# Hedgehog attention and a gated MLP on one core: one pool of PSUM banks, and the stages of a unit moved against each other

## The chip, the cores and the metric

One core of a Trainium2 chip runs the whole kernel in one launch. The metric is the device time of one execution in microseconds, as the median of several runs. TensorE (PE) multiplies matrices into PSUM; VectorE (DVE) and ScalarE (ACT) read PSUM and work elementwise; GpSimd (POOL) works on SBUF and issues the loads that convert fp32 to bf16; SyncE (SP) issues the other transfers.

## What is computed

The reference, cut to what matters (8 batches, 8 heads, 576 positions, 64 values per head, 128 features, all fp32):

```python
def phi(x):
    proj = x @ w_phi
    proj = proj - max(abs(proj), axis=-1)
    return concatenate([exp(proj), exp(-proj)])
kv  = einsum('bhsf,bhsd->bhfd', phi(k), v);  z = sum(phi(k), axis=2)
x   = (phi(q) @ kv) / (phi(q) @ z + 1e-06)         # heads side by side: (8, 576, 512)
h   = relu(x @ w_in);  u, v2 = h[..., :512], h[..., 512:]
v_s = w_spatial @ layernorm(v2) + b_spatial[:, None]
out = (u * v_s) @ w_out
```

## The kernel before

The 576 positions of a batch are 512 in four blocks of 128 and a rest of 64; the rests of two batches share one block. The attention is cut into 36 **units**: for each two batches one unit for their rests (a tail unit, all 8 heads), then four units per batch, each for two heads ("pairs"). Each unit goes through these stages, written as functions:

- `a_transpose` (L182): 8 transposes on TensorE of key and query blocks into one bank; ScalarE copies the key half to `kT` (L194), VectorE the query half to `qT` (L195), one after the other.
- `a_keys` (L204): the key features, two banks of `ps`. VectorE takes the largest magnitude, `mk` (L212), then ScalarE the exponentials `kf` (L215), four in all.
- `a_queries` (L217): the same product for the queries, of which only the largest magnitude `mq` is kept (L221).
- `a_scale` (L224): ScalarE makes `em` = exp(-mk), exp(mk) (L227); GpSimd multiplies the values by it into `vs` (L232, two instructions, and a small copy L234; L242 and L244 in a tail unit).
- `a_split` (L248): two small VectorE instructions write `mq` as a bf16 value (L250) and its remainder (L251) into `mhl`.
- `a_max_t` (L253): `mhl` is transposed (L255) and VectorE copies it to `mT` (L256).
- `a_qfeat` (L258): the query features transposed, less their maximum (L266 and L270, which reads `mT`), and their exponentials `qf` on ScalarE (L283).
- `a_kv` (L286): the key sums (L296, L298), copied to `kv` by VectorE (L300).
- `a_num` (L308): numerator and denominator (L315), then reciprocal and product on VectorE (L305, L306).
- `a_x_t` (L319): the result transposed (L324) and copied to `xT` (L325).

The MLP of a batch is a list of **fillers** made by `b_tasks` (L482), each about four wide matmuls and what reads them: `b_v` (L372: product, ReLU on ScalarE, statistics on VectorE L362), `b_ln` (L383: root on GpSimd, four normalisations L387), `b_u` (L403: product, ReLU on ScalarE), `b_s` (L423: spatial product, gate on VectorE L431), `b_o` (L456: product, copy on ScalarE L453, store). There are 160 of them in all. A batch's list enters the queue when `a_x_t` of its last unit is emitted.

The order is written out by hand in `step(i)` (L513): one call emits stages of up to four units, and `fill(0.25)` four times, each adding a quarter of RATE to a credit (at most 2) and emitting one filler per credit. From this order the building tool makes one program per engine, in which each engine works strictly in turn; it may change the order a little where it takes an instruction to be ready earlier. What is left in the queue after the last step is emitted at the end (L567), the **drain**.

Before, a step emits for the units u (this one), w, z, y (one, two, three before): transposes of u, fill, `mT` of w, key sums of w, keys of u, fill, `xT` of y, queries of u, query features of w, fill, numerators of z, scale and split of u, fill. PSUM has 8 banks, in four pools: 1 for every transpose (`ps_tr`), 3 for feature products (`ps_pj`), 2 for key sums and numerators (`ps_kn`), 2 for the MLP (`ps_s2`). The spatial weights are transposed on TensorE after units 4 and 5 (L157).

Loads with conversion are issued on GpSimd (L84, L97, L98, L121 to L124), the fp32 values on SyncE (L86, L99). The identity that every transpose needs is built on GpSimd (L108, L109; masks.py:197 and 199).

Of the kernel before, what the change touches and what calls it, by code (L numbers as in the profile page):

```python
# [16 lines left out]
def kernel(  # L17
# [15 lines left out]
    nc = tc.nc  # L33
# [24 lines left out]
    ps_tr = ctx.enter_context(tc.tile_pool(name="ps_tr", bufs=1, space=bass.MemoryType.PSUM))  # L58
    ps_pj = ctx.enter_context(tc.tile_pool(name="ps_pj", bufs=3, space=bass.MemoryType.PSUM))
    ps_kn = ctx.enter_context(tc.tile_pool(name="ps_kn", bufs=2, space=bass.MemoryType.PSUM))  # L60
    ps_s2 = ctx.enter_context(tc.tile_pool(name="ps_s2", bufs=2, space=bass.MemoryType.PSUM))
# [43 lines left out]
    nc.gpsimd.dma_start(out=wphi2[D:2 * D, F:2 * F], in_=w_phi)  # L105
    load_tail(0)
    load(0, parts=4)
    ident = cpool.tile([P, P], BF16)  # L108
    make_identity(nc, ident)  # L109
# [4 lines left out]
    wsp = cpool.tile([P, NB, S], BF16)  # L114
# [5 lines left out]
    def load_weights():  # L120
        nc.gpsimd.dma_start(out=w_in_bf, in_=moe_w_in.rearrange("(kc p) f -> p kc f", p=P))  # L121
        nc.gpsimd.dma_start(out=wsp, in_=moe_w_spatial[0:T0, :].rearrange("(p c) s -> p c s", c=NB))
# [34 lines left out]
    def transpose_spatial(i):  # L157

        pt = ps_tr.tile([P, S], BF16, tag="tr", name="pt")
# [9 lines left out]
        for bl in range(2):  # L169
            lo = bl * TL  # L170
            for tp, c in enumerate(POS):
                nc.tensor.transpose(out=pt[lo:lo + TL, tp * P:(tp + 1) * P], in_=wsp[:, c, T0:S], identity=ident)
# [9 lines left out]
    def a_transpose(u):  # L182
        src = st[u["b"]] if u["pair"] else gs[u["g"]]
        pt = ps_tr.tile([P, 2, 4, P], BF16, tag="tr", name="pt")
# [12 lines left out]
    def by_token(xT, half):  # L197
        ps = ps_pj.tile([P, 4, F], FP32, tag="pj", name="ps")
# [5 lines left out]
    def a_keys(u):  # L204
# [3 lines left out]
                            bufs=3 if u["pair"] else 2)  # L208
# [15 lines left out]
    def a_scale(u):  # L224
# [3 lines left out]
        if u["pair"]:  # L228
            pj = u["pj"]
            vs = feat.tile([P, 2, H, DS], BF16, tag="vs", name="vs", bufs=3)  # L230
# [22 lines left out]
    def a_max_t(u):  # L253
        pt = ps_tr.tile([P, P], BF16, tag="tr", name="pt")
        nc.tensor.transpose(out=pt, in_=mhl[u["i"] % NM], identity=ident)  # L255
        nc.vector.tensor_copy(out=mT[u["i"] % NM][0:2 * H, :], in_=pt[0:2 * H, :])  # L256

    def a_qfeat(u):  # L258
# [3 lines left out]
        for half in range(2):  # L262
            pq = ps_pj.tile([P, 4, P], FP32, tag="pj", name="pq")
# [14 lines left out]
            if u["pair"]:  # L278
                qf = feat.tile([P, 2, 4, P], BF16, tag="qf", name="qf", bufs=5)
# [6 lines left out]
    def a_kv(u):  # L286
# [4 lines left out]
        pv = ps_kn.tile([P, 2, 2, DA], FP32, tag="kn", name="pv")  # L291
# [16 lines left out]
    def a_num(u):  # L308
        d = st[u["b"]]
        u["x"] = a1.tile([P, NB, 2, D], BF16, tag="x", name="x", bufs=3)  # L310
        for hh in range(2):
            pn = ps_kn.tile([P, NB, DA], FP32, tag="kn", name="pn")
# [6 lines left out]
    def a_x_t(u):  # L319
        if u["pj"] == 0:  # L320
            st[u["b"]]["xT"] = s2.tile([P, KC, T0], BF16, tag="xT", name="xT", bufs=3)
        pt = ps_tr.tile([P, NB, P], BF16, tag="tr", name="pt")
# [4 lines left out]
    def tail_num(g, bls):  # L327
# [4 lines left out]
        for i in range(2):  # L332
            pn = ps_kn.tile([P, 4, DA], FP32, tag="kn", name="pn")
# [265 lines left out]
```

## Time and profile before

| | us |
|---|---|
| median of 3 runs | 374.42 |
| the runs | 373.71 to 376.15 |
| the profiled execution | 374.99 |
| its span in the trace | 373.2 |

| engine | busy us | share of the span |
|---|---|---|
| TensorE matmuls | 301.4 | 81% |
| VectorE | 280.4 | 75% |
| ScalarE | 235.1 | 63% |
| GpSimd | 138.5 | 37% |

The span runs from the first to the last instruction; the execution's time is 1.8 us longer. Matmuls overlap in their pipeline, so TensorE's busy time is somewhat more than its work. VectorE is called DVE in the rows, ScalarE ACT, GpSimd POOL.

### The profile page before, as it was taken

The numbers are of one execution on the slowest core, as the hardware profiler recorded it, in microseconds if no ns is written. First come the engines' busy times: TensorE is split into PE (matmuls) and PEld (weight loads), VectorE is DVE, ScalarE is ACT, GpSimd is POOL, SyncE is SP. The second block draws the span as 40 slices with busy tenths as digits, with TensorE's granted clock in tenths as the row PEclk, the third lists the DMA queues.
The fourth block names the chain that finished last, engine by engine and source line by source line (L and its number), as shares of the span: only waits on it lengthen the run. The fifth ranks groups of instructions, "written<-read, shape, count | busy, mean of one in ns | idle before, by whom it ended". The sixth has DMA issues, their size and how long they took to land.

```text
span 373.2 us, 8490 instructions
## 1 busy us (share of the span) xinstructions
PE 301.4 (81%) x3370; PEld 201.3 (54%) x3370; DVE 280.4 (75%) x696; ACT 235.1 (63%) x514; POOL 138.5 (37%) x198
## 2 busy tenths in 40 slices
PE   0176768796988799879787999897868998898995
PEld 0055656564655566546554667565536665554442
DVE  5288868898866988599987997788797985567260
ACT  3058635875677686777866667877776558651633
POOL 7669522454603632434425230635332222220010
PEclk9999879998999999999998999999999999999998
DMA  8999980088112931373009301990000003210303
GB/s 184 215 202 202 104 184 2 2 112 142 27 62 70 115 114 50 90 103 114 2 1 114 115 1 58 180 246 3 0 2 3 0 4 138 97 23 0 129 0 126
DMA packets 44460, 31.13 MB, mean 83 GB/s; under 512 B 14018, under 2 KB 39170, under 8 KB 44420
## 3 DMA queue, kind: packets, MB, share of 16 engines
q0 software_dynamic: 26624, 11.71, 25.4%
q1 hardware_dynamic: 17796, 18.88, 16.0%
q8 instruction: 26, 0.43, 0.5%
q14 instruction: 14, 0.11, 0.1%
HBM read 32.85 MB, written 9.44 MB: 113 GB/s over the span
## 4 chain that ended last, share of the span: by engine, by line
PE 23%; DVE 17%; ACT 13%; POOL 8%; DMA 4%; issue 3%; POOLq 0%; ACTq 0%; DVEq 0%; SPq 0%
ACT kf L215 5%; PE po L451 4%; ACT qf L283 4%; PE ps L428 4%; DMA out_dram<-ob 4%; DVE stats L362 3%; POOL vs L232 3%; DVE mk L212 3%; DVE vn L387 2%; PE pv L296 2%; POOL rstd L369 2%; PE ps L200 2%; ACT kT L194 1%; PE pv L359 1%; PE pq L266 1%
## 5 line engine op out<-in xcount | busy, mean ns | idle before, releaser
L215 ACT ACTIVATE kf<-ps 128x512 bf16<-128x512 f32 x144 | 75.0, 603 | 54.1 <-DVE mk L212 46.7
L232 POOL TENSOR_TENSOR vs<-v_f,em 128x512 bf16<-128x512 f32 x64 | 65.5, 1044 | 112.1 <-ACT em L227 109.0
L283 ACT ACTIVATE qf<-pq 128x512 bf16<-128x512 f32 x128 | 66.6, 621 | 7.8 <-PE pq L270 7.8
L221 DVE TENSOR_REDUCE mq<-ps 128x4 f32<-128x512 f32 x72 | 47.4, 678 | 3.0 <-PE ps L200 1.7
L212 DVE TENSOR_REDUCE mk<-ps 128x4 f32<-128x512 f32 x72 | 47.0, 675 | 1.1 <-PE ps L200 1.1
L296 PE MATMUL pv<-vs,kf 128*128 128x65 bf16 x512 | 26.2, 193 | 21.7 <-POOL vs L234 16.1
L296 PEld LDWEIGHTS <-kf 128*128 128x128 bf16 x512 | 24.1, 97 | 31.1 <-issue 27.1
L194 ACT COPY kT<-pt 128x512 bf16<-128x512 bf16 x36 | 22.3, 620 | 24.2 <-PE pt L191 24.2
L407 PE MATMUL pu<-xT,w_in_bf 128*128 128x512 bf16 x128 | 36.1, 395 | 0.6 <-ACT vr L361 0.6
L428 PE MATMUL ps<-w_spT,vn 128*128 128x512 bf16 x128 | 34.5, 379 | 1.7 <-ACT uTt L421 0.9
L361 ACT ACTIVATE vr<-pv 128x512 bf16<-128x512 f32 (+1 forms) x38 | 22.5, 616 | 18.5 <-PE pv L359 18.3
L362 DVE BATCH_NORM_STATS2 stats<-vr 128x6 f32<-128x512 bf16 (+1 forms) x38 | 25.4, 683 | 11.7 <-ACT vr L361 11.5
L453 ACT COPY ob<-po 128x512 f32<-128x512 f32 (+1 forms) x38 | 22.9, 613 | 17.5 <-PE po L451 10.0
L451 PE MATMUL po<-w_out_bf,uT 128*128 128x512 bf16 x128 | 33.0, 378 | 0.9 <-DVE uT L431 0.5
L359 PE MATMUL pv<-w_in_bf,xT 128*128 128x512 bf16 x128 | 32.5, 379 | 0.8 <-ACT vr L361 0.6
L200 PE MATMUL ps<-wphi,qT 128*128 128x256 bf16 x144 | 29.7, 291 | 3.4 <-ACT kf L215 2.7
L266 PE MATMUL pq<-qT,wphi 128*128 128x256 bf16 x128 | 30.7, 276 | 1.6 <-DVE mq L221 1.3
L270 PE MATMUL pq<-mT,sel 128*128 128x128 bf16 x256 | 30.5, 221 | 0.0
L270 PEld LDWEIGHTS <-sel 128*128 128x128 bf16 x256 | 25.2, 99 | 6.4 <-issue 3.1
L200 PE MATMUL ps<-wphi,kT 128*128 128x256 bf16 x144 | 25.9, 297 | 2.9 <-ACT kT L194 2.9
L431 DVE TENSOR_TENSOR uT<-ps,uT 128x512 bf16<-128x512 f32 x32 | 21.8, 684 | 7.5 <-PE ps L429 7.5
L409 ACT ACTIVATE uT<-pu 128x512 bf16<-128x512 f32 x32 | 19.7, 626 | 10.8 <-PE pu L407 10.8
(107 smaller groups left out, 623.2 us busy)
## 6 DMA issues: line engine op xcount, KB each, us to landing
v_f<-in_v_dram SPq DMA_DIRECT2D x8, 1024.0 KB, 6.8
out_dram<-ob SPq DMA_DIRECT2D x32, 256.0 KB, 2.4
k_bf<-in_k_dram POOLq DMA_DIRECT2D x7, 512.0 KB, 6.5
q_bf<-in_q_dram POOLq DMA_DIRECT2D x7, 512.0 KB, 7.6
v_tl<-in_v_dram SPq DMA_DIRECT2D x8, 128.0 KB, 10.6
w_in_bf<-in_moe_w_in_dram POOLq DMA_DIRECT2D x1, 1024.0 KB, 13.2
out_dram<-ob SPq DMA_DIRECT2D x8, 128.0 KB, 2.3
wsp<-in_moe_w_spatial_dram POOLq DMA_DIRECT2D x1, 576.0 KB, 15.3
```

What stands on the lines that cost most here:

```text
L200: nc.tensor.matmul(out=ps[:, 2 * x:2 * x + 2, :], lhsT=xT[:, 2 * half + x, :], rhs=wphi2, start=True, stop=True)
L212: nc.vector.tensor_reduce(out=u["mk"][:, hs], in_=pk, axis=AX.X, op=ALU.max, apply_absolute_value=True)
L215: nc.scalar.activation(out=u["kf"][:, s, hs, :], in_=pk, func=AF.Exp, bias=0.0, scale=sc)
L221: nc.vector.tensor_reduce(out=u["mq"][:, 4 * half:4 * half + 4], in_=pq, axis=AX.X, op=ALU.max, apply_absolute_value=True)
L232: nc.gpsimd.tensor_tensor(out=vs[:, s, :, 0:D], in0=st[u["b"]]["v"][:, pj * H:(pj + 1) * H, :], in1=em[:, s, :].unsqueeze(2).to_broadcast( ...
L270: nc.tensor.matmul(out=pq[:, 2 * par + x, :], lhsT=sel[:, j, :], rhs=m, start=False, stop=(x == 1))
L283: nc.scalar.activation(out=qf[:, s], in_=pq, func=AF.Exp, bias=0.0, scale=sc)
L296: nc.tensor.matmul(out=pv[:, hh, s, :], lhsT=u["kf"][:, s, 4 * hh + c, :], rhs=u["vs"][:, s, 4 * hh + c, 0:DA], start=(c == 0), stop=False)
L359: nc.tensor.matmul(out=pv[r], lhsT=lhs(kc), rhs=w_in_bf[:, kc, HALF:DFF], start=(kc == 0), stop=(kc == KC - 1))
L362: nc.vector.bn_stats(out=stats[r], in_=dst[r])
L428: nc.tensor.matmul(out=ps, lhsT=d["vn"][:, sp, cs], rhs=w_spT[:, sp, 0:T0], start=(sp == 0), stop=False)
L451: nc.tensor.matmul(out=po[r], lhsT=lhs(dc), rhs=w_out_bf[:, dc, :], start=(dc == 0), stop=(dc == KC - 1))
```

## The change

All PSUM tiles come from one pool with one tag and eight buffers, handed out in turn. `step` emits stages of up to six units, n (the next one) to x (four before): keys and scale of u, fill, key sums of z (two before; until now one before), queries and split of u, fill, transposes of n, `mT` of w, fill, `xT` of x, query features of w, fill, numerators of y. So the transposes come one step earlier, and the key sums, the numerators, `xT` and with it a batch's fillers one step later; there is one step more. RATE falls from 4.4 to 4.0. `kf`, `vs` and `qf` get one, one and two buffers more; the spatial weights use a buffer of `vn` until that is needed, and their last 64 columns are a load of their own. The identity is built ahead of the first loads.

```diff
-    ps_tr = ctx.enter_context(tc.tile_pool(name="ps_tr", bufs=1, space=bass.MemoryType.PSUM))
-    ps_pj = ctx.enter_context(tc.tile_pool(name="ps_pj", bufs=3, space=bass.MemoryType.PSUM))
-    ps_kn = ctx.enter_context(tc.tile_pool(name="ps_kn", bufs=2, space=bass.MemoryType.PSUM))
-    ps_s2 = ctx.enter_context(tc.tile_pool(name="ps_s2", bufs=2, space=bass.MemoryType.PSUM))
+    psum = ctx.enter_context(tc.tile_pool(name="psum", bufs=8, space=bass.MemoryType.PSUM))
...
+    ident = cpool.tile([P, P], BF16)
+    make_identity(nc, ident)
     load_tail(0)
     load(0, parts=4)
-    ident = cpool.tile([P, P], BF16)
-    make_identity(nc, ident)
...
-    wsp = cpool.tile([P, NB, S], BF16)
+    wsp = s2.tile([P, NB, T0], BF16, tag="vn", name="wsp", bufs=3)
+    wspr = cpool.tile([P, NB, TL], BF16)
...
-        nc.gpsimd.dma_start(out=wsp, in_=moe_w_spatial[0:T0, :].rearrange("(p c) s -> p c s", c=NB))
+        rows = moe_w_spatial[0:T0, :].rearrange("(p c) s -> p c s", c=NB)
+        nc.gpsimd.dma_start(out=wsp, in_=rows[:, :, 0:T0])
+        nc.gpsimd.dma_start(out=wspr, in_=rows[:, :, T0:S])
...
-                nc.tensor.transpose(out=pt[lo:lo + TL, tp * P:(tp + 1) * P], in_=wsp[:, c, T0:S], identity=ident)
+                nc.tensor.transpose(out=pt[lo:lo + TL, tp * P:(tp + 1) * P], in_=wspr[:, c, :], identity=ident)
...
-        pt = ps_tr.tile([P, 2, 4, P], BF16, tag="tr", name="pt")
+        pt = psum.tile([P, 2, 4, P], BF16, tag="bank", name="pt")
...
-        ps = ps_pj.tile([P, 4, F], FP32, tag="pj", name="ps")
+        ps = psum.tile([P, 4, F], FP32, tag="bank", name="ps")
...
-                            bufs=3 if u["pair"] else 2)
+                            bufs=4 if u["pair"] else 2)
...
-            vs = feat.tile([P, 2, H, DS], BF16, tag="vs", name="vs", bufs=3)
+            vs = feat.tile([P, 2, H, DS], BF16, tag="vs", name="vs", bufs=4)
...
-                qf = feat.tile([P, 2, 4, P], BF16, tag="qf", name="qf", bufs=5)
+                qf = feat.tile([P, 2, 4, P], BF16, tag="qf", name="qf", bufs=7)
...
-    RATE = 4.4
+    RATE = 4.0
...
     def step(i):
-        u, w, z, y = unit(i), unit(i - 1), unit(i - 2), unit(i - 3)
+        n, u, w, z, y, x = (unit(i + d) for d in (1, 0, -1, -2, -3, -4))
+        if i == 0:
+            a_transpose(u)
         if u:
-            a_transpose(u)
+            a_keys(u)
+            a_scale(u)
         fill(0.25)
+        if z and z["pair"]:
+            a_kv(z)
+        if u:
+            a_queries(u)
+            a_split(u)
+        fill(0.25)
+        if n:
+            a_transpose(n)
         if w:
             a_max_t(w)
-        if w and w["pair"]:
-            a_kv(w)
-        if u:
-            a_keys(u)
+        fill(0.25)
+        if x and x["pair"]:
+            a_x_t(x)
+            if x["pj"] == NP - 1:
+                g, bl = x["g"], x["b"] % 2
+                alone = g in SPLIT
+                if alone or bl == 1:
+                    tail_x_t(g, [bl] if alone else [0, 1])
+                queue.extend(b_tasks(x["b"]))
+        if w:
+            a_qfeat(w)
         fill(0.25)
         if y and y["pair"]:
-            a_x_t(y)
+            a_num(y)
             if y["pj"] == NP - 1:
                 g, bl = y["g"], y["b"] % 2
                 alone = g in SPLIT
                 if alone or bl == 1:
-                    tail_x_t(g, [bl] if alone else [0, 1])
-                queue.extend(b_tasks(y["b"]))
-        if u:
-            a_queries(u)
-        if w:
-            a_qfeat(w)
-        fill(0.25)
-        if z and z["pair"]:
-            a_num(z)
-            if z["pj"] == NP - 1:
-                g, bl = z["g"], z["b"] % 2
-                alone = g in SPLIT
-                if alone or bl == 1:
                     tail_num(g, [bl] if alone else [0, 1])
-        if u:
-            a_scale(u)
-            a_split(u)
-        fill(0.25)
-
-    for i in range(NU + 3):
+
+    def on_pair(i):
+        u = unit(i)
+        return u if u and u["pair"] else None
+
+    for i in range(NU + 4):
         u = unit(i)
         step(i)
         if i == 0:
```

The same edit from the four old pools to `psum.tile(..., tag="bank")` stands at every PSUM tile. `on_pair` is not called.

**Three places in the engines' programs.** First GpSimd at the very start; `k_tl` and `q_tl` are the rest blocks of the first two batches, `k_bf` and `q_bf` full blocks. Before:

```order
L98 DMA q_bf<-in_q_dram 128x2x256
L97 DMA k_bf<-in_k_dram 128x2x256
L98 DMA q_bf<-in_q_dram 128x2x256
masks.py:197 MEMSET ident 128x128
L97 DMA k_bf<-in_k_dram 128x8x256
masks.py:199 ISA
masks.py:199 AFFINE_SELECT ident<-ident 128x128
L98 DMA q_bf<-in_q_dram 128x8x256
L121 DMA w_in_bf<-in_moe_w_in_dram 128x4x1024
```

Now:

```order
L599 UNCONDITIONAL_BRANCH
masks.py:197 MEMSET ident 128x128
L81 DMA k_tl<-in_k_dram 64x8x64
L101 DMA wphi_76<-in_w_phi_dram 64x128
L102 DMA wphi_76<-in_w_phi_dram 64x128
masks.py:199 ISA
masks.py:199 AFFINE_SELECT ident<-ident 128x128
L81 DMA k_tl<-in_k_dram 64x8x64
L81 DMA q_tl<-in_q_dram 64x8x64 x2
L94 DMA k_bf<-in_k_dram 128x2x256
```

The identity moved ahead of all loads but one; behind the loads of batch 1, where `w_in_bf` and the spatial weights were issued before, the tail unit's `vst` now comes first.

Second, VectorE through one unit in the middle, while gates (`uT`, a filler's work) are due. Before:

```order
L212 TENSOR_REDUCE mk<-ps 128x4 x2
L325 COPY xT<-pt 128x512
L221 TENSOR_REDUCE mq<-ps 128x4 x2
L305 RECIPROCAL rc<-pn 128x4 x2
L306 TENSOR_TENSOR x<-pn,rc 128x4x64 x2
L250 CAST mhl_129<-mq 128x8
L251 TENSOR_TENSOR mhl_129<-mq,mhl_129 128x8
L431 TENSOR_TENSOR uT<-ps,uT 128x512
L195 COPY qT<-pt 128x512
L431 TENSOR_TENSOR uT<-ps,uT 128x512
L256 COPY mT_131<-pt 16x128
```

Now:

```order
L212 TENSOR_REDUCE mk<-ps 128x4 x2
L431 TENSOR_TENSOR uT<-ps,uT 128x512
L300 CAST kv<-pv 128x4x65
L221 TENSOR_REDUCE mq<-ps 128x4 x2
L431 TENSOR_TENSOR uT<-ps,uT 128x512
L250 CAST mhl_129<-mq 128x8
L195 COPY qT<-pt 128x512
L251 TENSOR_TENSOR mhl_129<-mq,mhl_129 128x8
L256 COPY mT_127<-pt 16x128
```

The reciprocals and products (`rc`, `x`) stood between `mq` and the two split instructions (`mhl`) and now come after `mT`, outside this piece; `kv` moved up between `mk` and `mq`. In all 35 units that can be compared `mT` stood behind `qT`; now it does in 16 of 34, as here, and ahead of it in 18.

Third, ScalarE through one unit. Before:

```order
L215 ACTIVATE kf<-ps 128x512 x4
L453 COPY ob<-po 128x512
L283 ACTIVATE qf<-pq 128x512 x4
L453 COPY ob<-po 128x512
L227 ACTIVATE em<-mk 128x8 x2
```

Now:

```order
L215 ACTIVATE kf<-ps 128x512 x4
L227 ACTIVATE em<-mk 128x8 x2
L409 ACTIVATE uT<-pu 128x512
L421 ACTIVATE uTt<-pu 128x4x64
L194 COPY kT<-pt 128x512
L283 ACTIVATE qf<-pq 128x512 x4
```

In 14 of the 36 units other instructions stood between the key exponentials (`kf`) and `em`, for which GpSimd waits, in nine of them the query exponentials (`qf`) as here; now `em` follows `kf` directly in all 36.

## Rows read from the trace of the kernel before

**Rows 1.** Busy us by stretch: length, then PE, PEld, DVE, ACT, POOL; granted clock, DMA, GB/s.
```profile
18.30:84.40 66.10, 51.40 (x590) 38.37 (x590) 55.53 (x126) 44.21 (x101) 34.99 (x49) 0.92 0.79 115
84.40:315.50 231.10, 201.01 (x2377) 137.05 (x2377) 189.54 (x474) 161.93 (x362) 82.81 (x115) 0.99 0.31 69
315.50:373.20 57.70, 48.01 (x397) 25.05 (x395) 27.96 (x72) 25.92 (x50) 8.32 (x14) 0.98 0.20 69
```

**Rows 2.** Timeline of ScalarE, the copy of a transposed key block (L194).
```profile
18.30 0.58 ACT L194 COPY kT<-pt 128x512 bf16<-128x512 bf16 x1 [14.56 <-PE pt L191]
...
84.41 0.62 ACT L194 COPY kT<-pt 128x512 bf16<-128x512 bf16 x1
...
315.48 0.72 ACT L194 COPY kT<-pt 128x512 bf16<-128x512 bf16 x1
```

**Rows 3.** Who VectorE waited for, 84.4 to 315.5 us: total us, times, longest.
```profile
DVE qT L195 <- ACT kT L194: 10.5, 11, 3.4
DVE mT L256 <- PE pt L255: 5.6, 9, 1.6
```

**Rows 4.** Who TensorE waited for in the same stretch.
```profile
PE pv L296 <- POOL vs L234: 8.5, 7, 2.3
```

**Rows 5.** Timeline of the start, GpSimd and then TensorE; columns: start us, us, engine, line.
```profile
14.85 0.71 POOL L98 DMA_DIRECT2D q_bf<-in_q_dram  x1 [0.67 <-DMA q_tl<-in_q_dram]
...
16.89 0.30 POOL masks.py:199 TENSOR_SCALAR_AFFINE_SELECT ident<-ident 128x128 bf16<-128x128 bf16 x1
...
18.84 0.55 POOL L122 DMA_DIRECT2D wsp<-in_moe_w_spatial_dram  x1
...
26.83 0.26 POOL L244 CAST vst<-em 64x16 bf16<-64x16 f32 x1
17.25 0.58 PE L191 MATMUL pt<-ident,k_tl 128*128 128x128 bf16 x4 [17.25 <-POOL ident masks.py:199]
```

**Rows 6.** DMA issues on the page: count, KB each, us to landing.
```profile
wsp<-in_moe_w_spatial_dram POOLq DMA_DIRECT2D x1, 576.0 KB, 15.3
```

**Rows 7.** Groups by line: busy us, mean ns of one, then idle before.
```profile
L362 DVE BATCH_NORM_STATS2 stats<-vr 128x6 f32<-128x512 bf16 (+1 forms) x38 | 25.4, 683 | 11.7 <-ACT vr L361 11.5
...
L250 DVE CAST mhl<-mq 128x8 bf16<-128x8 f32 x36 | 17.7, 492 | 0.4
...
L251 DVE TENSOR_TENSOR mhl<-mq,mhl 128x8 bf16<-128x8 f32 x36 | 15.7, 435 | 0.7
```

**Rows 8.** All instructions of L250 and of L251: ns minimum/median/maximum.
```profile
L250 DVE CAST mhl<-mq x36: 154/204/2226, 22.8 to 321.7; 128x8 bf16<-128x8 f32 x36
L251 DVE TENSOR_TENSOR mhl<-mq,mhl x36: 130/168/1000, 23.6 to 321.9; 128x8 bf16<-128x8 f32 x36
```

**Rows 9.** Timeline of one unit in mid-run: VectorE, ScalarE, GpSimd.
```profile
219.27 0.43 DVE L300 CAST kv<-pv 128x260 bf16<-128x260 f32 x1
219.62 1.28 DVE L212 TENSOR_REDUCE mk<-ps 128x4 f32<-128x512 f32 x2
...
225.09 0.42 DVE L306 TENSOR_TENSOR x<-pn,rc 128x256 bf16<-128x256 f32 x1
...
220.33 2.06 ACT L215 ACTIVATE kf<-ps 128x512 bf16<-128x512 f32 x4 [2.39 <-DVE mk L212]
...
222.57 2.04 POOL L232 TENSOR_TENSOR vs<-v_f,em 128x512 bf16<-128x512 f32 x2 [6.00 <-ACT em L227]
```

**Rows 10.** Timeline of one unit near the start, VectorE and then GpSimd.
```profile
33.16 2.23 DVE L250 CAST mhl<-mq 128x8 bf16<-128x8 f32 x1
...
33.28 2.07 POOL L232 TENSOR_TENSOR vs<-v_f,em 128x512 bf16<-128x512 f32 x2
```

**Rows 11.** Timeline of TensorE near the end.
```profile
321.23 0.27 PE L266 MATMUL pq<-qT,wphi 128*128 128x256 bf16 x1
...
322.11 0.66 PE L315 MATMUL pn<-kv,qf 128*128 128x65 bf16 x16
...
345.16 3.63 PE L451 MATMUL po<-w_out_bf,uT 128*128 128x512 bf16 x16 [0.27 <-DVE uT L431]
```

More of the change, by code (lines that the diff above doesn't have):

```diff
@@ L157, in transpose_spatial @@
     def transpose_spatial(i):
-        pt = ps_tr.tile([P, S], BF16, tag="tr", name="pt")
+        pt = psum.tile([P, S], BF16, tag="bank", name="pt")
         if i < NB:
@@ L253, in a_max_t @@
     def a_max_t(u):
-        pt = ps_tr.tile([P, P], BF16, tag="tr", name="pt")
+        pt = psum.tile([P, P], BF16, tag="bank", name="pt")
         nc.tensor.transpose(out=pt, in_=mhl[u["i"] % NM], identity=ident)
@@ L262, in a_qfeat @@
         for half in range(2):
-            pq = ps_pj.tile([P, 4, P], FP32, tag="pj", name="pq")
+            pq = psum.tile([P, 4, P], FP32, tag="bank", name="pq")
             if u["pair"]:
@@ L290, in a_kv @@
         ut = dg["unit"]
-        pv = ps_kn.tile([P, 2, 2, DA], FP32, tag="kn", name="pv")
+        pv = psum.tile([P, 2, 2, DA], FP32, tag="bank", name="pv")
         for hh in range(2):
@@ L311, in a_num @@
         for hh in range(2):
-            pn = ps_kn.tile([P, NB, DA], FP32, tag="kn", name="pn")
+            pn = psum.tile([P, NB, DA], FP32, tag="bank", name="pn")
             for pos in range(NB):
@@ L321, in a_x_t @@
             st[u["b"]]["xT"] = s2.tile([P, KC, T0], BF16, tag="xT", name="xT", bufs=3)
-        pt = ps_tr.tile([P, NB, P], BF16, tag="tr", name="pt")
+        pt = psum.tile([P, NB, P], BF16, tag="bank", name="pt")
         for pos in range(NB):
@@ L332, in tail_num @@
         for i in range(2):
-            pn = ps_kn.tile([P, 4, DA], FP32, tag="kn", name="pn")
+            pn = psum.tile([P, 4, DA], FP32, tag="bank", name="pn")
             for y in range(4):
@@ L348, in tail_x_t @@
         r = slice(bls[0] * TL, (bls[-1] + 1) * TL)
-        pt = ps_tr.tile([P, KC, P], BF16, tag="tr", name="pt")
+        pt = psum.tile([P, KC, P], BF16, tag="bank", name="pt")
         for kc in range(KC):
@@ L356, in v_mm @@
     def v_mm(lhs, dst, r, stats, mv):
-        pv = ps_s2.tile([P, HALF], FP32, tag="s2", name="pv")
+        pv = psum.tile([P, HALF], FP32, tag="bank", name="pv")
         for kc in range(KC):
@@ L404, in b_u @@
         d = st[b]
-        pu = ps_s2.tile([P, T0], FP32, tag="s2", name="pu")
+        pu = psum.tile([P, T0], FP32, tag="bank", name="pu")
         for kc in range(KC):
@@ L415, in b_u_tail @@
         r = slice(bls[0] * TL, (bls[-1] + 1) * TL)
-        pu = ps_s2.tile([P, KC, P], FP32, tag="s2", name="pu")
+        pu = psum.tile([P, KC, P], FP32, tag="bank", name="pu")
         for dc in range(KC):
@@ L424, in b_s @@
         d = st[b]
-        ps = ps_s2.tile([P, T0], FP32, tag="s2", name="ps")
+        ps = psum.tile([P, T0], FP32, tag="bank", name="ps")
         cs = slice(dc * P, (dc + 1) * P)
@@ L434, in b_s_tail @@
         d = gs[g]
-        ps = ps_s2.tile([P, KC, 2, TL], FP32, tag="s2", name="ps")
+        ps = psum.tile([P, KC, 2, TL], FP32, tag="bank", name="ps")
         for dc in range(KC):
@@ L448, in o_mm @@
     def o_mm(lhs, r):
-        po = ps_s2.tile([P, DM], FP32, tag="s2", name="po")
+        po = psum.tile([P, DM], FP32, tag="bank", name="po")
         for dc in range(KC):
```

## The prediction

> **What bounds the kernel now.** I read the copies of the key block first, because each marks the start of a unit's keys: the tail unit's at 18.3, the tenth unit's at 84.4, the last unit's at 315.5 us [rows 2]. These cut the span into a start, a start-up with few fillers, a steady part of 26 units (231.1 / 26 = 8.89 us each) and an end. The busy times by stretch come next [rows 1]. In the steady part TensorE is busy for 201.0 of 231.1 us (87%) and VectorE for 189.5 (82%), ScalarE for 70%: no engine is full, so the units' handovers set the pace, and VectorE and TensorE share the floor. In the end TensorE has 48.0 of 57.7 us and VectorE 28.0, so there TensorE sets the time. Then the waits: VectorE stood 10.5 us at `qT` for ScalarE's copy and 5.6 us at `mT` [rows 3]; TensorE stood 8.5 us at the key sums for GpSimd's `vs` [rows 4]. The sum below goes by VectorE through start-up and steady part, and by TensorE in the end.
>
> **Start.** The last of the tail's query blocks has landed by 14.85 us, where GpSimd's wait for it ends; the first transpose waits until 17.25 us for the identity [rows 5]. With the identity built ahead, the load issues slip by its two pieces, 0.30 us for the one shown and as much for its memset, an estimate: 14.85 + 0.6 = 15.45. From the first transpose to the key copy it took 18.30 - 17.25 = 1.05 us, so that copy comes at 16.5 us, 1.8 earlier. What is late next is the load itself. It cannot gain over 2.4 (17.25 - 14.85), and loses nothing unless the loads slip by over 2.4.
>
> **Start-up.** Up to the tenth unit VectorE was busy for 55.5 us in 66.1 [rows 1]. The fillers now begin a step later and the transposes come a step earlier, so of the seven fillers that stood here none is left. They hold five statistics and four normalisations, some ten instructions at 0.68 us [rows 7] with the small ones, 6.5 us. That leaves 49.0. Of the 10.6 us idle I keep 6.5, since without fillers nothing stands beside a unit's own chain; 3 and 10.6 are the ends. The tenth copy then falls at 16.5 + 49.0 + 6.5 = 72.0 instead of 84.4.
> The spatial weights are issued behind the tail's `vst` now, which ended near 27.1 us [rows 5]; 1.8 earlier and behind `w_in_bf` that makes some 26 instead of 18.8, and with 15.3 us to landing [rows 6] 41. Five units at about 5.5 us from 16.5 put their first use at 42 to 44, so I take nothing; a stall there of up to 4 us stays in the range, and TensorE, in order, would hold every stage behind it.
>
> **Steady part: fillers.** By the rule of credits 107 fillers were emitted between these two copies, and now 103. Of seventeen fillers of a batch the VectorE instructions are four statistics, four normalisations and four gates, 12 x 0.68 / 17 = 0.5 us per filler. So VectorE has 189.5 - 2 = 187.5 us of today's work.
>
> **Steady part: the port.** The two split instructions last 0.492 and 0.435 us in the mean but 0.204 and 0.168 in the median [rows 7, 8]: 0.56 us per unit is standing. One of 2.23 us lies beside GpSimd's 2.07 us of `vs`, and both end together [rows 10]. `vs` began 222.57 - 219.62 = 2.95 us after the first `mk` and lasted 2.04 [rows 9]. Now `em` always follows `kf` directly, and on VectorE the split comes after `mk`, `kv` and `mq`, with 1.28 + 0.43 + 1.28 (`mq` taken as `mk`) = 3.0 us of work: it arrives just as `vs` begins. Before, `rc` and `x` stood between, or `em` was late, and many pairs missed it. The ends are a pair that always misses (27 x -0.56 = -15) and one that always stands as the worst did, 2.23 + 0.17 - 0.93 = 1.47 more, 27 x 1.47 = +40. I take +0.6 per unit, +16 us, nearer to the mean than to the worst, because fillers still shift the pair.
> The Trainium skill (SBUF — State Buffer, "Who interferes with whom") speaks against the change here: a VectorE cast in its two-port mode and a GpSimd instruction lock each other out of a shared pair of ports for a whole instruction, and a VectorE instruction with two SBUF inputs contends with GpSimd's reads too. The trace agrees, as the 2.23 beside 2.07 us shows [rows 10]. By that rule alone, with every pair in the window, the case is the second rival below.
>
> **Steady part: what VectorE waits for.** It was idle for 231.1 - 189.5 = 41.6 us. The waits at `qT` and `mT` are 16.1 of it [rows 3]. The transposes have half a step's lead now, and `mT` no longer stands behind `qT` in 18 of 34 units, so I take 12 of the 16.1 away. While VectorE stands at the port the others catch up: of the 29.6 left I let the 16 added us swallow 15.6, and 14 us remain. Ends: 5, and 35 if the handovers only change places. TensorE's waits for `vs` [rows 4] end too, as the key sums come a step later; with VectorE as the floor that is worth nothing more.
> The one pool adds a wait: a bank comes round after eight tiles, and TensorE, in order, holds transposes, features, numerators and fillers behind it, and so VectorE and ScalarE. No row shows such a ring. Its price lies between nothing and one pair of exponentials per unit (2.06 / 2 = 1.03 [rows 9], 27.8 us); I take nothing, because a unit with its fillers takes 16 banks, so that eight are half a unit's time, over 4 us, and a bank's readers need 0.64 + 1.03 for two exponentials behind `mk`.
> Together 187.5 + 16 + 14 = 217.5 us, 8.37 per unit.
>
> **End.** After the last key copy 46 fillers were left, now 57. A wide product takes 3.63 / 4 = 0.91 us [rows 11], and TensorE sets the time here: 57.7 + 11 x 0.91 = 67.7. The ends are 64 and 70.
>
> **The sum.** 72.0 + 217.5 + 67.7 = 357.2 of span, and 1.8 outside it: 359.0 against the profiled 374.99. The median stands 0.6 below that, so 358.4; I forecast 358.
>
> **Rivals.**
> 1. The port costs no more than today and VectorE is fed almost without a gap. For it: eight banks and a full step of lead. Against it: the order that puts the pair at the window. Start-up 70, steady 187.5 + 13, end 67.7, 1.8, less 0.6: 339.
> 2. The port takes everything: +40, with 5 us of idle left, is 232.5 in the steady part; 72.0 + 232.5 + 67.7 + 1.8 - 0.6 = 373. For it speaks the match of 3.0 and 2.95 us; against it that fillers come between. A cadence that does not change at all comes to much the same, 372.
> 3. Slower: a closed loop through five instruction streams. Where `mT` stands behind the split, it waits for the end of `vs`, 2.95 + 2.04 = 4.99 us after `mk` [rows 9]; then the second split instruction 0.17, query features and numerators 322.11 + 0.66 - 321.23 = 1.54 [rows 11], a filler 0.91, two products 0.84 [rows 9], and the next `mk`: 8.45, with handovers near 8.9, and 9.6 when a second filler's product stands in TensorE's way. It decides from about 18 units of 26 at 9.6: 18 x 9.6 + 8 x 8.37 = 240, and 72.0 + 240 + 67.7 + 1.2 = 381. Against it: `mT` stands ahead of `qT` in half the units.
>
> **How the numbers follow.** Forecast 0.50, first rival 0.25, second 0.15, third 0.10. About 1% can be told from no change (runs 373.7 to 376.2). The forecast's own spread, steady 206 to 228, is 347 to 369, faster throughout; the first rival is faster too; the second falls within 1% but for 0.04 on its fast side; of the third 0.02 falls within 1%. Faster 0.79, same 0.13, slower 0.08. The range reaches down to the first rival and up over the second: 338 to 374.
>
> **What would show it.** In the profile after: first key copy near 16.5, tenth near 72, last near 290 us; VectorE's idle time between the last two under 20 us; the means of the split instructions together near 1.5 us instead of 0.93; no wait for `vs` at the key sums; an end of 66 to 69 us. A tenth copy after 78, a cadence of 8.8 or more, or TensorE waiting for banks by over 10 us in total would make it wrong.

## The result and the profile after

The changed kernel takes 346.25 us in the median of 4 runs (344.78 to 347.78), the kernel before 374.06: a ratio of 0.925, 95% interval 0.919 to 0.930, 28 us faster. Forecast were 358 us in a range of 338 to 374. The profiled execution took 347.78 us and its span is 346.0, against 374.99 and 373.2.

The copies of the key block cut the span as before: the first, the tenth, the eleventh and the last (rows 2 had the first, tenth and last). Columns: start, us, engine, line, idle before.

```profile
15.56 0.58 ACT L194 COPY kT<-pt 128x512 bf16<-128x512 bf16 x1 [11.83 <-PE pt L191]
...
61.59 0.58 ACT L194 COPY kT<-pt 128x512 bf16<-128x512 bf16 x1 [0.94 <-PE pt L255]
73.84 0.62 ACT L194 COPY kT<-pt 128x512 bf16<-128x512 bf16 x1
...
278.55 0.58 ACT L194 COPY kT<-pt 128x512 bf16<-128x512 bf16 x1 [0.21 <-PE pt L255]
```

The engines' busy times by stretch, in the columns of [rows 1], after:

```profile
15.50:61.60 46.10, 35.90 (x487) 28.73 (x486) 41.87 (x100) 36.63 (x86) 34.49 (x48) 0.96 1.19 169
61.60:278.50 216.90, 193.19 (x2306) 133.22 (x2303) 182.85 (x473) 164.15 (x367) 86.06 (x120) 0.98 0.34 71
278.50:346.00 67.50, 62.03 (x576) 34.00 (x573) 37.56 (x99) 31.30 (x58) 8.43 (x14) 1.00 0.21 71
```

Of the 27.2 us of span the start gave 2.7 (18.30 to 15.56), the start-up 20.1 (66.1 to 46.0), the steady part 14.1 (231.1 to 217.0), and the end took 9.8 back (57.7 to 67.5). The tenth copy flatters the start-up somewhat, since a unit's transposes now stand in the step of the unit before it and the gap from the tenth to the eleventh is 12.3 us. By the eleventh copy (95.57 before, 73.84 now) start and start-up together gave 21.7 and the 25 units behind it 15.2 (8.80 to 8.19 us a unit). In the steady part TensorE now has 193.2 of 216.9 us, 89%, VectorE 182.9, 84% (87 and 82% before). Over the whole span TensorE's idle time fell by 18.1 us (71.8 to 53.7) and its busy time by 9.1 (301.4 to 292.3); both make up the 27.2.

Who TensorE waited for in the steady part, after ([rows 4] before; total, times, longest):

```profile
PE pq L270 <- DVE mT L256: 4.1, 7, 1.0
PE ps L200 <- DVE qT L195: 3.0, 3, 2.2
PE pv L359 <- DVE mq L221: 1.7, 1, 1.7
PE pq L266 <- ACT kf L215: 1.6, 4, 0.6
PE pv L359 <- ACT kf L215: 1.3, 1, 1.3
```

The wait for `vs`, 8.5 us before, is gone from the head of the list. The last three rows show what the ring of banks looks like: the filler's product `pv` waits for `mq`, and the query features for `kf`, which are none of their operands but read the bank that they are to write. Added up over the whole span, such waits for a reader are 16.6 us, 36 of them; with the four pools of before they were 24.9, 43 of them.

VectorE in the same stretch, after ([rows 3] before):

```profile
DVE rc L305 <- PE pn L315: 9.8, 8, 2.1
DVE stats L362 <- ACT vr L361: 5.2, 4, 2.5
DVE vn L387 <- POOL rstd L369: 4.2, 4, 1.9
DVE qT L195 <- ACT kT L194: 3.6, 4, 1.4
```

`qT` fell from 10.5 to 3.6 and `mT` left the list; now it waits longer for products of TensorE. Before, from 84.4 to 315.5 us, this row was:

```profile
DVE rc L305 <- PE pn L315: 4.1, 8, 1.3
```

The chain of work that ended last, followed back from the last instruction, lies on VectorE for longer than on TensorE. Its shares of the span by engine, after:

```profile
DVE 41%; PE 35%; ACT 8%; POOL 7%; DMA 4%; issue 2%; POOLq 0%; SPq 0%; ACTq 0%
```

### The profile page after: what moved, and what is told of

The parts are those of the page before. It is cut to its first block, busy times and chain, and to the rows that moved or that the text cites. A ratio compares the mean times of both kernels' runs of the same rounds, so it can differ in the third digit from the quotient of the medians.

```text
span 346.0 us, 8470 instructions
## 1 busy us (share of the span) xinstructions
PE 292.3 (84%) x3370; PEld 196.6 (57%) x3370; DVE 269.5 (78%) x696; ACT 235.1 (68%) x514; POOL 139.2 (40%) x199
## 4 chain that ended last, share of the span: by engine, by line
DVE 41%; PE 35%; ACT 8%; POOL 7%; DMA 4%; issue 2%; POOLq 0%; SPq 0%; ACTq 0%
PE po L451 9%; DVE mk L212 7%; DVE mq L221 6%; DVE stats L362 4%; PE ps L428 4%; ACT kf L215 4%; PE pu L407 4%; DVE x L306 4%; PE ps L200 3%; DVE uT L431 3%; PE pq L270 3%; DMA q_tl<-in_q_dram 3%; DVE mhl L250 3%; DVE mhl L251 3%; DVE vn L387 2%; POOL rstd L369 2%
## 5 line engine op out<-in xcount | busy, mean ns | idle before, releaser
L215 ACT ACTIVATE kf<-ps 128x512 bf16<-128x512 f32 x144 | 76.3, 623 | 25.5 <-DVE mk L212 24.9
L221 DVE TENSOR_REDUCE mq<-ps 128x4 f32<-128x512 f32 x72 | 46.0, 676 | 0.0
L407 PE MATMUL pu<-xT,w_in_bf 128*128 128x512 bf16 x128 | 34.3, 393 | 3.8 <-DVE x L306 1.2
L453 ACT COPY ob<-po 128x512 f32<-128x512 f32 (+1 forms) x38 | 22.9, 606 | 20.8 <-issue 12.5
L266 PE MATMUL pq<-qT,wphi 128*128 128x256 bf16 x128 | 31.7, 274 | 4.3 <-DVE kv L300 2.1
L270 PE MATMUL pq<-mT,sel 128*128 128x128 bf16 x256 | 28.0, 222 | 5.5 <-DVE mT L256 5.5
L451 PE MATMUL po<-w_out_bf,uT 128*128 128x512 bf16 x128 | 31.8, 379 | 0.1
L194 ACT COPY kT<-pt 128x512 bf16<-128x512 bf16 x36 | 22.2, 617 | 13.9 <-PE pt L191 11.8
L200 PE MATMUL ps<-wphi,kT 128*128 128x256 bf16 x144 | 23.6, 280 | 7.0 <-ACT kT L194 3.2
L270 PEld LDWEIGHTS <-sel 128*128 128x128 bf16 x256 | 22.9, 99 | 11.5 <-issue 9.2
L315 PEld LDWEIGHTS <-qf 128*128 128x128 bf16 x512 | 20.4, 97 | 11.0 <-issue 6.3
L306 DVE TENSOR_TENSOR x<-pn,rc 128x256 bf16<-128x256 f32 x64 | 25.4, 416 | 0.5
```

What stands on the lines that cost most here:

```text
L200: nc.tensor.matmul(out=ps[:, 2 * x:2 * x + 2, :], lhsT=xT[:, 2 * half + x, :], rhs=wphi2, start=True, stop=True)
L215: nc.scalar.activation(out=u["kf"][:, s, hs, :], in_=pk, func=AF.Exp, bias=0.0, scale=sc)
L221: nc.vector.tensor_reduce(out=u["mq"][:, 4 * half:4 * half + 4], in_=pq, axis=AX.X, op=ALU.max, apply_absolute_value=True)
L270: nc.tensor.matmul(out=pq[:, 2 * par + x, :], lhsT=sel[:, j, :], rhs=m, start=False, stop=(x == 1))
L306: nc.vector.tensor_tensor(out=x, in0=pn[r, :, 0:D], in1=rc[r].to_broadcast([n, 4, D]), op=ALU.mult)
L407: nc.tensor.matmul(out=pu, lhsT=w_in_bf[:, kc, dc * P:(dc + 1) * P], rhs=d["xT"][:, kc, :], start=(kc == 0), stop=(kc == KC - 1))
```

## The experiments

The ratios are to the kernel before, beside which each ran; its median was 374.4 to 376.2 us in these comparisons. A kernel made from the one before with one pool has line numbers 3 lower than those quoted so far, the new order with four pools 3 higher.

**One pool, nothing else.** In the kernel before only the four pools are replaced, by the change's own line, and every PSUM tile takes its bank from there.

```diff
-    ps_tr = ctx.enter_context(tc.tile_pool(name="ps_tr", bufs=1, space=bass.MemoryType.PSUM))
...
+    psum = ctx.enter_context(tc.tile_pool(name="psum", bufs=8, space=bass.MemoryType.PSUM))
...
-        pt = ps_tr.tile([P, 2, 4, P], BF16, tag="tr", name="pt")
+        pt = psum.tile([P, 2, 4, P], BF16, tag="bank", name="pt")
```

> The kernel before with nothing changed but the PSUM pools: one pool of eight banks. Theory order: the gain comes from the lead of the transposes and the later key sums, and banks alone bring under 8 us (366 to 374). Theory banks: the single bank for all transposes was the stall, mT no longer stands behind qT, and the pool alone brings half of the 28 us or more (360 or below).

Measured 405.36 us, ratio 1.077 [1.070, 1.084]: 30 us slower, where neither theory had a loss. TensorE's waits, in an execution of 411.1 us, the longest of four:

```profile
PE pv L293 <- POOL vs L231: 42.2, 21, 4.8
PE pt L252 <- DVE mhl L248: 22.0, 11, 5.4
```

And one place of TensorE's timeline in it:

```profile
211.96 0.22 PE L252 MATMUL pt<-ident,mhl 128*128 128x128 bf16 x1
214.66 0.29 PE L293 MATMUL pv<-vs,kf 128*128 128x65 bf16 x4 [2.49 <-POOL vs L231]
...
215.29 0.60 PE L197 MATMUL ps<-wphi,kT 128*128 128x256 bf16 x4
```

The key sums stand where `step` writes them, ahead of the next unit's own keys (L197), and TensorE holds those for `vs`. In this kernel's program of TensorE the stages of every unit stand in the written order; with four pools the building tool had moved them past each other, and the wait for `vs` was 8.5 us in the steady part [rows 4], 16.1 over the span. This span, 409.3 us, exceeds the one before by 36.1: by 26.5 of TensorE's idle time and 9.6 of its busy time, 311.0 against 301.4 us, at a granted clock of 0.912 against 0.975. The Trainium skill (Perfetto Trace Analysis, "Matmuls") asks that independent groups rotate through different banks, so that one is emptied while the next is filled. The trace has nothing against that, but the run shows that rotation through all eight is no gain by itself.

**The new order, four pools.** In the changed kernel only the pools are those of before.

```diff
-    psum = ctx.enter_context(tc.tile_pool(name="psum", bufs=8, space=bass.MemoryType.PSUM))
+    ps_tr = ctx.enter_context(tc.tile_pool(name="ps_tr", bufs=1, space=bass.MemoryType.PSUM))
...
-        pt = psum.tile([P, 2, 4, P], BF16, tag="bank", name="pt")
+        pt = ps_tr.tile([P, 2, 4, P], BF16, tag="tr", name="pt")
```

> The changed kernel with the four old pools (1, 3, 2, 2 banks). Theory order: most of the gain stays, 348 to 354. Theory banks: transposes, mT and xT wait for one bank again and the time goes back to 362 or above. If both are needed together, this and the pool alone both stay above 360.

Measured 379.19 us, ratio 1.011 [1.007, 1.015]. One row of TensorE's waits carries it:

```profile
PE pt L258 <- DVE qT L198: 22.4, 19, 3.6
```

The transposes of the split means find the one bank for transposes still occupied by a block that VectorE has not copied (5.7 us before). So the pool alone costs 30 us, the rest of the change without the pool some 4, and both together gain 28, as the last sentence of the expectation has it: no part's gain can be read from the part alone.

**Key sums one step earlier.** The changed kernel with the key sums of w, as before, in place of z.

```diff
-        if z and z["pair"]:
-            a_kv(z)
+        if w and w["pair"]:
+            a_kv(w)
```

> The changed kernel with the key sums of the unit one before (as in the kernel before) instead of two before, at the same place of the step; all else as changed. Theory a: a lead of a step over GpSimd's vs is enough and the later key sums are worth under 4 us (346 to 350). Theory b: vs ends too late for the next step and TensorE stands for it again, over 10 us in total; the time is 354 or more.

Measured 358.94 us, ratio 0.954 [0.948, 0.960], 12.7 us over the changed kernel, as the second theory has it. The wait for `vs` is back:

```profile
PE pv L296 <- POOL vs L234: 10.0, 3, 5.3
```

Most of the loss is in the start-up: the tenth key copy comes at 70.83 instead of 61.59, the last at 291.06 instead of 278.55.

**Transposes in their own step.** The changed kernel with a unit's transposes at the head of its own step, a filler and the key sums between them and its keys.

```diff
-        if i == 0:
+        if u:
             a_transpose(u)
-        if u:
-            a_keys(u)
-            a_scale(u)
         fill(0.25)
         if z and z["pair"]:
             a_kv(z)
         if u:
+            a_keys(u)
+            a_scale(u)
             a_queries(u)
             a_split(u)
         fill(0.25)
-        if n:
-            a_transpose(n)
```

> The changed kernel with the transposes of a unit back in its own step, with a filler and the key sums between them and the keys; key sums two steps later as changed, one pool. Theory a: the lead of the transposes is what the order is worth, because ScalarE gets to the key copy only behind its exponentials: TensorE waits for kT by 1 us per unit or more and the time is 360 or above. Theory b: the lead matters little beside the key sums: under 352.

Measured 365.35 us, ratio 0.972 [0.965, 0.979], 19 us over the changed kernel:

```profile
PE ps L200 <- DVE qT L195: 14.3, 7, 5.1
PE ps L200 <- ACT kT L194: 11.3, 14, 1.4
```

Here TensorE stands for the copies that follow the transposes. Ahead by half a step, these two waits are 3.5 and 3.2 us over the span of the changed kernel. But the filler and the key sums, now ahead of the keys, no longer stand between keys and queries; how much of the 14.3 us at `qT` comes of that was not tried.

**Scale and split at the end of the step.** The changed kernel with `a_scale` and `a_split` in the places that they had before.

```diff
             a_keys(u)
-            a_scale(u)
...
             a_queries(u)
-            a_split(u)
...
+        if u:
+            a_scale(u)
+            a_split(u)
```

> The changed kernel with the scaling and the split of a unit at the end of its step, where they stood before. Theory a (port): the split pair leaves the window of vs less often or more often, and the time moves by at most 4 us. Theory b (chain): em comes behind the query exponentials, vs and mhl come half a step later, and the time rises by over 10 us; that would explain most of what the pool alone costs.

Measured 347.28 us, ratio 0.924 [0.917, 0.930]: the same as the changed kernel within the interval. Yet the split's two groups, which the prediction had put at the port, shrank. In this run (busy us, mean ns):

```profile
L250 DVE CAST mhl<-mq 128x8 bf16<-128x8 f32 x36 | 14.7, 409 | 0.2
...
L251 DVE TENSOR_TENSOR mhl<-mq,mhl 128x8 bf16<-128x8 f32 x36 | 11.0, 305 | 0.6
```

Nine microseconds less of them on VectorE than in the changed kernel bought nothing. That does not free VectorE of being the floor, since the split also comes later here: TensorE now waits 4.5 us for `mhl`, a row that the changed kernel does not have. The chain that ended last moved to TensorE (in the changed kernel it was 41% on VectorE):

```profile
PE 45%; DVE 23%; ACT 17%; POOL 7%; issue 3%; DMA 3%; POOLq 0%; ACTq 0%
```

**More fillers per step.** The changed kernel with the old rate.

```diff
-    RATE = 4.0
+    RATE = 4.4
```

> The changed kernel with RATE at 4.4 as before. The end shortens by about one 0.9 us filler for each of some 10 fillers (from 67.5 to near 58), the steady part takes them instead: if TensorE, 90% busy there, is the bound, the sum stays within 2 us; if it has room beside VectorE, 3 to 8 us faster; if VectorE is the bound and fillers disturb the units, 2 to 5 us slower.

Measured 347.93 us, ratio 0.931 [0.925, 0.937]. The last key copy came at 281.45 instead of 278.55, and the end took 64.6 instead of 67.5 us: fillers move from the end into the steady part and the sum stays, as would be expected where TensorE is nearly full in both. The expectation's ten fillers and 58 us were wrong: the end has 15 fewer of the 512-wide products, some four fillers.

**Identity behind the loads.** The changed kernel with the identity where it was.

```diff
-    ident = cpool.tile([P, P], BF16)
-    make_identity(nc, ident)
     load_tail(0)
     load(0, parts=4)
+    ident = cpool.tile([P, P], BF16)
+    make_identity(nc, ident)
```

> The changed kernel with the identity built again behind the loads of the first batch. If the start is worth what the two traces show (first key copy at 15.56 instead of 18.30 us), this run is 2 to 3 us slower than the changed kernel and its first key copy lies near 18.3; if VectorE's later work swallows the lead, it is under 1 us slower.

Measured 347.73 us, ratio 0.927 [0.922, 0.931]. The first key copy is 3.1 us later (18.67), the sixth 1.9 (40.73 against 38.86), the tenth 1.2, the thirteenth 0.3 earlier. The lead is real. How much of it the kernel itself swallows isn't shown: this execution was granted the full clock up to the thirteenth copy, that of the changed kernel 0.93 of it up to the sixth and 0.94 from the tenth to the thirteenth. In the latter stretch TensorE's waits are the same in both but for 0.1 us, and the 1.4 us between them are its busy time, 22.2 us here and 23.6 there. At the end at most 1.5 us of the lead are left, within the spread of the runs.

**Six and seven banks.** The changed kernel with a shorter ring, 6 or 7 in place of 8.

```diff
-    psum = ctx.enter_context(tc.tile_pool(name="psum", bufs=8, space=bass.MemoryType.PSUM))
+    psum = ctx.enter_context(tc.tile_pool(name="psum", bufs=7, space=bass.MemoryType.PSUM))
```

> The changed kernel with six buffers in the one pool instead of eight. The prediction took the ring of eight as free, since its banks come round after half a unit and their readers need under 2 us: then six cost at most 4 us (346 to 350). If the ring already decides when TensorE may go on, six cost 10 us or more and TensorE's waits for readers of PSUM grow by as much.

> The changed kernel with seven banks in its pool in place of eight. Six banks cost 13 us. Theory a (TensorE sets the time and the ring only has to be long enough): most of the loss comes with the second bank taken away, and seven cost at most 4 us: 345 to 350. Theory b (each bank counts alike): half of the thirteen, 352 to 354, with the waits of TensorE for readers about half-way between.

Measured 359.35 us for six, ratio 0.958 [0.951, 0.965], and 353.57 for seven, ratio 0.943 [0.939, 0.947]: 13.1 and 7.3 us over eight. So each bank counts about alike, and a slope that has not flattened at eight suggests that eight still limit something; a ninth can't be had. TensorE's waits for a reader of its bank, added up, are 30.4 us with six (in the longest of its four executions, 363.1 us), 19.7 with seven, 16.6 with eight. The 10.7 more from seven to six cover that step's 5.8 us; the 3.1 more from eight to seven do not cover its 7.3, and where the rest went stays open.

**The pool alone, its two waits moved behind.** Back to the kernel before with one pool, and two of its stages moved within their step, from ahead of the keys to behind the queries.

```diff
-        if w:
-            a_max_t(w)
-        if w and w["pair"]:
-            a_kv(w)
...
         if u:
             a_queries(u)
+        if w:
+            a_max_t(w)
+        if w and w["pair"]:
+            a_kv(w)
```

> The kernel before with one pool of eight banks, and in its step the transposes of the split means and the key sums moved from ahead of the unit's own keys to behind its queries; transposes, scaling and split stand where they stood. With the pool alone TensorE stood 42.2 us at the key sums for the scaled values (16.1 before) and 22.0 us at the split means (2.3 before), 46 us more at two places, and the time was 30 us longer. Theory a (one ring makes the compiler keep the written order, and the written order of before has those two waits at the head of every step): with the two places moved behind 2 to 3 us of other work both waits fall below 10 us and the time comes back to 365 to 385. Theory b (the ring itself: banks of long-lived tiles held up the next ones, wherever the two stand): the time stays at 395 to 410 and the lost time turns into waits of TensorE for readers of banks or into waits elsewhere.

Measured 356.57 us, ratio 0.951 [0.947, 0.955]: 49 us faster than the pool alone, by four moved lines, 18 faster than before, and 8 under the window that the first theory had given. Who TensorE waits for now:

```profile
PE ps L197 <- ACT kT L191: 21.1, 23, 2.0
...
PE pv L293 <- POOL vs L231: 2.4, 2, 2.3
```

The wait for `mhl` has left the list. One place of its timeline: queries (L197), split means, key sums and query features follow without a gap.

```profile
203.25 0.60 PE L197 MATMUL ps<-wphi,qT 128*128 128x256 bf16 x4
203.69 0.22 PE L252 MATMUL pt<-ident,mhl 128*128 128x128 bf16 x1
203.75 0.29 PE L293 MATMUL pv<-vs,kf 128*128 128x65 bf16 x4
...
204.38 0.38 PE L263 MATMUL pq<-qT,wphi 128*128 128x256 bf16 x2
```

That the ring itself was the cost falls with this run. The loss lay in two places of the old order, which stands as written with one ring. Whether these four lines would gain as much with the four pools was not tried; the new order did not (379.19 us).

**Only the key sums behind.** As the run above, but the split means stay at the head of the step.

```diff
-        if w and w["pair"]:
-            a_kv(w)
...
             a_queries(u)
+        if w and w["pair"]:
+            a_kv(w)
```

> As the run before it in this call, but only the key sums are moved behind the queries; the transposes of the split means stay at the head of the step. Theory a: the wait for scaled values (42.2 us with the pool alone) falls below 10 us, that for the split means stays at about 20 us or grows, since nothing of the key sums stands behind it any longer, and the time is between: 375 to 395. Theory b (the ring itself): 395 to 410 as with the pool alone.

Measured 368.93 us (364.51 to 372.18), ratio 0.980 [0.972, 0.988]. Of the 49 us the key sums, moved first, are worth 36 and the split means then 12; the wait for `mhl` stays as expected, and the time is 6 us under the expected window:

```profile
PE pt L252 <- DVE mhl L248: 18.5, 10, 4.3
...
PE pv L293 <- POOL vs L231: 6.0, 4, 3.6
```

**And the transposes ahead.** The pool with both waits behind the queries, and the next unit's transposes ahead of them.

```diff
+        if i == 0:
+            a_transpose(u)
-        if u:
-            a_transpose(u)
...
             a_queries(u)
+        if n:
+            a_transpose(n)
         if w:
             a_max_t(w)
```

> The kernel before with one pool of eight banks, split means and key sums behind the queries (356.57 us), and now also the transposes of the next unit ahead of them in the same place. The key sums still belong to the last unit, not the one before it, and stay beside the query features; identity, buffers and rate stay as before. In the run it builds on TensorE stood 21.1 us, 23 times, at the own keys for the copy of the transposed keys, which follows the transposes directly. Theory a (what the changed kernel won beyond that run comes from the transposes ahead, and the key sums need no whole step of delay): that wait falls below 6 us, and the time is 345 to 351, beside 346 for the changed kernel. Theory b (the key sums one step later are needed for the rest): the waits for scaled values come back or the next waits take the place, and the time stays at 353 to 360.

Measured 351.42 us, ratio 0.937 [0.933, 0.941], 0.4 us outside the window of the first theory. The wait for `kT` went as expected, from 21.1 to this:

```profile
PE ps L197 <- ACT kT L191: 1.9, 2, 1.2
```

Of those 19 us only 5 came off the time; in their place TensorE stands 5.2 us at the query features for `kf` and 4.9 at its transposes for `x`, which it hardly did in the run before. Five more lie between this kernel and the changed one, in which the key sums, numerators and `xT` come a whole step later, scale and split stand earlier in it, the buffers are more, the identity stands ahead and the rate is 4.0. The waits for `vs` are 5.7 us here and 0.6 in the changed kernel; how much of the five that is was not tried alone. No run came out faster than the changed kernel beyond the spread.

## Why the prediction was right, and where its steps were not

The direction and the range held; the median came 12 us under the forecast, most of it by the start-up. Of the signs that were put down, the wait for `vs` (0.6 us over the span), the cadence (8.3 us a unit) and the end came true. Tenth and last copy (61.6 and 278.6 against 72 and 290 us), VectorE's idle time (34.1 against under 20), the split's means (0.967 against 1.5) and the waits for banks (16.6 against 10) did not.

**Start.** Forecast 16.5, measured 15.56. The loads did not slip: the tail's keys were transposed as they landed, and so were its queries.

```profile
14.95 0.58 PE L191 MATMUL pt<-ident,q_tl 128*128 128x128 bf16 x4 [2.69 <-DMA q_tl<-in_q_dram]
```

The prediction had counted 1.05 us from the first transpose to the key copy, keys and queries together; with the keys done earlier it took 15.56 - 14.95 = 0.61. So the gain, 2.7 us, passed the 2.4 that were called its limit. The step held, and the run with the identity behind shows that it is worth 1.5 us or less at the end.

**Start-up.** Forecast for the tenth copy 72.0 from 49.0 us of VectorE and 6.5 idle; measured 61.59 from 41.9 and 4.2. By the fairer mark, the eleventh copy, 72.0 + 8.4 = 80.4 was forecast and 73.84 measured: 6.5 too late, 0.9 of them from the start. The term that was mis-sized is VectorE's work, "that leaves 49.0": between the first and the eleventh copy it fell from 64.2 us in 149 instructions to 50.8 in 125, 13.4 us less where 6.5 had been taken off for fillers. Of the 24 instructions that left this stretch, by the groups of both traces, nine are the fillers' (6.3 us, as put down), one is set-up, and 14 are stages of the units themselves (7.0 us), which now lie later with respect to the key copy: eight of the numerators, two of `xT`, two of the split and one each of `kv` and `mT`. The prediction had left these out. The spatial weights did no harm, as put down: issued at 25.0 us, landed 11.6 later, first used at 38.9.

**Steady part.** Forecast 217.5, measured 217.0, by two errors that cancel. The sum said 203.5 us of VectorE's work and 14 idle; it was 182.85 and 34.1.

The port was priced at +16 us. The two groups after, beside [rows 7] (0.492 and 0.435), and their spread, beside [rows 8]:

```profile
L251 DVE TENSOR_TENSOR mhl<-mq,mhl 128x8 bf16<-128x8 f32 x36 | 18.8, 522 | 0.1
L250 DVE CAST mhl<-mq 128x8 bf16<-128x8 f32 x36 | 16.0, 445 | 0.2
```

```profile
L250 DVE CAST mhl<-mq x36: 150/170/2452, 19.4 to 288.6; 128x8 bf16<-128x8 f32 x36
...
L251 DVE TENSOR_TENSOR mhl<-mq,mhl x36: 144/684/1015, 19.6 to 288.8; 128x8 bf16<-128x8 f32 x36
```

The means add up to 0.967 us a unit, against 0.927 before and 1.5 forecast: 27 x 0.04 = +1 us. The pair does meet `vs` more often (in the timelines, L250 overlaps GpSimd's products in 25 of 36 units and L251 in 23, before in some 23 and 16), but the standing moved from the first instruction to the second, as the medians show, and the meeting costs less there. One unit, VectorE and then GpSimd:

```profile
203.73 0.16 DVE L250 CAST mhl<-mq 128x8 bf16<-128x8 f32 x1
...
204.13 0.69 DVE L251 TENSOR_TENSOR mhl<-mq,mhl 128x8 bf16<-128x8 f32 x1
```

```profile
202.75 2.04 POOL L232 TENSOR_TENSOR vs<-v_f,em 128x512 bf16<-128x512 f32 x2 [5.53 <-ACT em L227]
```

The cast begins near the seam of the two `vs` instructions (202.75 + 2.04 / 2 = 203.77) and lasts 0.16 us; L251, which reads two operands in SBUF, ends at 204.82 with the second of them at 204.79. The Trainium skill (SBUF — State Buffer, "Who interferes with whom") has both kinds of contention, which the prediction had cited; the trace agrees with it on the second in kind. What weight it has for the time, the run with scale and split late does not settle, since 9 us less of it came together with a later split. Meanwhile the normalisations got out of GpSimd's way (two of their 14 groups in the timeline overlap it, before seven of 11), from 0.590 us each to this, 5.1 us less over the span:

```profile
L387 DVE TENSOR_SCALAR vn<-vr,mv,rstd 128x512 bf16<-128x512 bf16 x32 | 11.9, 430 | 7.1 <-POOL rstd L369 7.1
```

The idle time was put at 14 us because VectorE was taken for the floor. The waits at `qT` and `mT` did go, 16.1 to 3.6 and less (12 were forecast); what grew are `rc` behind TensorE's numerators, 4.1 to 9.8 us, and the statistics behind ScalarE, 2.5 to 5.2. So the step that failed is "the sum below goes by VectorE through start-up and steady part": VectorE's work fell to 182.85 us and a further 34.1 were not filled. TensorE has 89% of this stretch, and of the 14 us gained there 7.8 are its busy time (201.0 to 193.2, with 71 matmuls fewer) and 6.4 its idle time. That TensorE alone sets the time is not shown either: with the chain at 41% on VectorE and 35% on TensorE, handovers between the two set it. The rival that gave the port everything fell with the measured 1 us, the closed loop through `vs` with 8.3 us a unit in place of its 9.6. The first rival had the port right and the idle time wrong, 34.1 us for its 13.

**The ring.** "I take nothing" held only beside what it replaced: eight banks cost TensorE 16.6 us of waits for readers, over the 10 us at which the prediction would have called itself wrong. That test was badly chosen, for the four pools had 24.9. The argument for nothing (eight banks are half a unit's time) falls with the slope of 5.8 and 7.3 us from six to seven to eight. What was not seen at all is what the pool does to the order: by itself it costs 30 us, with every unit's stages in the written order, and the new order gains only together with it.

**End.** Forecast 67.7, measured 67.5, with TensorE at 62.0 of it: the sum for the 11 fillers, 10.0 us, came true. It did so partly by luck: TensorE's busy time there grew by 14.0 us (48.0 to 62.0), since later stages of the units lie there too, and its idle time fell by 4.2 (9.7 to 5.5). With the higher rate, which leaves fewer fillers, the end is 64.6.

## What to carry over

With a shared ring of banks TensorE's program here kept the written order: before replacing separate pools by one, look in each step for the instructions that wait for another engine (here key sums for GpSimd, split means for VectorE) and put work of TensorE's own ahead of them. Four lines moved within a step were worth 49 us of the 405. Test such a pair of edits together and apart, because each alone can lose, and do not read the floor from a busy share: here two engines at 89 and 84% hand work to each other, and the forecast by one of them had both its work and its idle time wrong.

## What was not expected of the hardware

The same 3370 matmuls were busy for 301.4 us before and 292.3 after, at a mean granted clock of 0.975 and 0.985. The products of the queries alone (L200) fell from 29.7 to 22.9 us for 144 instructions, with the mean of one at 291 and 281 ns: the groups now follow another group directly and overlap with it in the pipeline, so it seems that TensorE's busy time depends on the order as well. That the overlap is the cause is argued from the timeline, not tested. And the kernels in which TensorE stood longest at one place, the start aside, were granted less of the clock: 0.912 to 0.932 in the four executions of the pool alone (where a wait lasts up to 5.4 us), 0.939 to 0.967 with only the key sums moved (4.3 us), 0.988 to 0.995 with both moved (2.5 us). That the waits are the cause is not shown. So some 20 of the 49 us between the first and the last of these kernels are TensorE's busy time, 311.0 against 290.3 us in the two traces (the second lacks the records of 42 matmuls).
